# Operands and weight buffers at chosen byte offsets, another DMA order in the prologue, and two more warm-up matmuls

## The chip, the cores and the metric

The kernel runs on one core of a Trainium2 chip. The metric is the device time of one execution in microseconds (us): the median of three runs was 606.72 us, between 606.63 and 608.52. The profile was taken from another execution, which took 604.41 us.

## The reference

Attention with a soft cap over 2 x 12 heads, then two feed-forward layers over the 896 tokens, all in float32 (the weights come as float64):

```
scores = scale * (q @ k.T)                   # 448 x 448 per head, head size 64
scores = cap * tanh(scores / cap)
attn   = exp(scores - max); attn /= (sum(attn) + 1e-9)
x      = attn @ v                            # as 896 tokens x 768
x      = (x @ w_a) * (x @ w_b) @ w_out       # 768 -> 1536 -> 768
h      = max(x @ w_in, 0)                    # 768 -> 2048
out    = (h * h) @ w_out2                    # 2048 -> 768
```

## The kernel before

**Prologue.** q and k of the first of 12 pairs of heads (`qk0`), the scalar cap (`craw`), `qk1` of the second pair and the first weight unit are loaded; six matmuls on a tile of zeros (`wacc`, L517) run meanwhile. Then come the first scores, from `qk0` (L51, L57), and their Tanh (L527, L528), whose factor `c1` VectorE makes from the scalar. The engines branch on the size of the cap, and the first of two bodies runs.

**Attention.** For each pair the body computes the scores and Tanh of the next pair (L51, L57, L226, L237), Exp (L257), the product with v (L235, L270) and the sums of the exponentials (L276, L278). Each float32 matmul stands as two in the trace. The normalised result is split into two float32r tiles, a high part and the low rest, so that three float32r products give nearly float32 accuracy.

**The feed-forward layers** are 408 weight blocks of 128 x 128. For one block, `mm` (L173, L175, L177) issues six matmuls of 448 columns: the high weights with the low operand, the low weights with the high operand, and both high parts, each for the two halves of the tokens. TensorE loads 128 x 128 weights before each. The operands are the tiles x0 to x5 (144 blocks), g0 to g11 (72), y0 to y5 (96) and h0 to h14 with `hlast` (96), one operand tile per block; this gives four stages. Accumulators take turns in PSUM (`sc`, `sc`, `pd`).

**Weights.** Six blocks make a unit. A unit is loaded as float64 into one of three buffers `raw`, turned into float32 (`nar`) by VectorE and ScalarE, and split into high and low parts in one of four buffers `whl`; `tick` does this three units ahead. All engines work through their instructions in the order in which they are written; semaphores hold them back where data is missing. SP issues nearly all DMAs, in the order of its queue.

**Where tiles lie.** Tiles are laid one after the other within each partition. The tiles of the left side (th0, qk1, raw, hlast, nar, whl, then x and later y) start 32 bytes past a multiple of 256, since their sizes (12544, 3584, 6144, 7168, 3072 bytes) are multiples of 256 themselves. Those of the right side (g, and later h) are laid from the top and start 224 bytes past one.

Of the kernel before, what the change touches and what calls it, by code (L numbers as in the profile page):

```python
# [8 lines left out]
F32 = mybir.dt.float32  # L9
F32R = mybir.dt.float32r  # L10
# [7 lines left out]
B, H, S, D = 2, 12, 448, 64  # L18
DM = H * D
FF1, FF2 = 1536, 2048  # L20
P = 128
# [6 lines left out]
KD = DM // P  # L28
NF1 = FF1 // P
NF2 = FF2 // P  # L30
UB = 6
UC = UB * P
RAWB, NARB, HLB = 3, 2, 4
AHEAD = 3
WARM = 6
LOAD_AT = (0, 1, 2, 6)
CONV_AT = ((7, 8), (9,), (10,), (11,), (12,), (13, 14), (15, 16), (17,), (18,), (19,), (20,), ())
WTOP = 122876.0
EPS = 1e-9
CAP_BITS = 0x42200001  # L40
# [2 lines left out]
def f32(ap):  # L43
    return ap.bitcast(F32)
# [15 lines left out]
def fetch(nc, raws, wu, u):  # L60
    t = raws[u % RAWB]
    src = wu[u]
    if wu.dtype != F32:
        src = src.bitcast(I32).rearrange("p (n t) -> p n t", t=2)
    nc.sync.dma_start(out=t, in_=src)
    return t


def body(ctx, tc, qk, v, wu, out, c1, cabs, guard, dscr, qk1, kept, bounded):
    nc = tc.nc  # L70
    ax = ExitStack()
# [11 lines left out]
    wp = ctx.enter_context(tc.tile_pool(name="wp", bufs=1))  # L83

    th0, h_last, raws = kept
    raw_t, hl_t = {0: raws[0]}, {}
    NU = wu.shape[0]
    wide = wu.dtype != F32
    pos = {"load": 1}

    def load_units(n):
        while pos["load"] < min(n, NU):
            raw_t[pos["load"]] = fetch(nc, raws, wu, pos["load"])
            pos["load"] += 1
# [3 lines left out]
    def conv(u, step, alone=False):  # L98
        if not 0 <= u < NU:
            return  # L100
        if step == 1:
            nar_t[u] = raw_t[u]
        if step == 6:
            hl = wp.tile([P, 2, UC], F32R, tag="whl", name="whl", bufs=HLB)
            if alone:
                nc.vector.tensor_copy(hl[:, 0], nar_t[u])
            else:
                nc.scalar.activation(out=hl[:, 0], in_=nar_t[u], func=AF.Copy)  # L108
            hl_t[u] = hl
        elif step == 7:  # L110
            raw_t.pop(u)
            hl = hl_t[u]
            nc.vector.tensor_tensor(out=hl[:, 1], in0=nar_t.pop(u), in1=f32(hl[:, 0]), op=ALU.subtract)  # L113
        elif not wide:
            return
        elif step == 1:
            t = wp.tile([P, UC], F32, tag="nar", name="nar", bufs=NARB)
            nc.vector.tensor_scalar(out=t, in0=raw_t[u][:, :, 1].bitcast(F32), scalar1=WTOP, scalar2=-WTOP, op0=ALU.min, op1=ALU.max)  # L118
            nar_t[u] = t
        elif step == 2:  # L120
            t = nar_t[u]
            if alone:
                nc.vector.tensor_scalar(out=t, in0=t, scalar1=2.0 ** -112, scalar2=None, op0=ALU.mult)
            else:
                nc.scalar.activation(out=t, in_=t, func=AF.Copy, scale=2.0 ** -112)  # L125
        else:
            r, t = raw_t[u], nar_t[u].bitcast(I32)
            if step == 3:
                nc.vector.tensor_scalar(out=t, in0=t, scalar1=3, scalar2=None, op0=ALU.logical_shift_left)  # L129
            elif step == 4:  # L130
                nc.vector.scalar_tensor_tensor(out=t, in0=r[:, :, 0], scalar=29, in1=t, op0=ALU.logical_shift_right, op1=ALU.bitwise_or)  # L131
            elif step == 5:
                nc.vector.scalar_tensor_tensor(out=t, in0=r[:, :, 1], scalar=-(1 << 31), in1=t, op0=ALU.bitwise_and, op1=ALU.bitwise_or)  # L133
# [45 lines left out]
    def split(dst, src):  # L179
        pend.append(("A", lambda: nc.scalar.activation(out=dst[:, 0], in_=src, func=AF.Copy)))  # L180
        pend.append(("V", lambda: nc.vector.tensor_tensor(out=dst[:, 1], in0=src, in1=f32(dst[:, 0]), op=ALU.subtract)))

    xs = ExitStack()
    xpool = xs.enter_context(tc.tile_pool(name="xpool", bufs=1, side="left"))
    xhl = [xpool.tile([P, 2, B, S], F32R, name=f"x{i}") for i in range(KD)]

    ap = ax.enter_context(tc.tile_pool(name="ap", bufs=1, side="right"))

# [13 lines left out]
    def gtile():  # L202
        gbuf.append(gbuf.pop(0))
        return gbuf[-1]
# [136 lines left out]
    def steps(j):  # L341
        for n in CONV_AT[j]:
            conv(n // 7, n % 7 + 1, True)
# [75 lines left out]

    gx = ExitStack()  # L420
    gp = gx.enter_context(tc.tile_pool(name="gp", bufs=1, side="right"))
    ghl = [gp.tile([P, 2, B, S], F32R, name=f"g{i}") for i in range(NF1)]
    split(ghl[0], g0)
    tick(1)
    for f in range(1, NF1):
        ab = (acc(), acc())
        g = gtile()
# [8 lines left out]
    xs.close()  # L436
    yx = ExitStack()
    yp = yx.enter_context(tc.tile_pool(name="yp", bufs=1, side="left"))
    yhl = [yp.tile([P, 2, B, S], F32R, name=f"y{i}") for i in range(KD)]
    for o in range(KD):  # L440
        a = acc()
        for kk in range(NF1):
# [4 lines left out]
    gx.close()  # L447
    hx = ExitStack()
    hpool = hx.enter_context(tc.tile_pool(name="hp", bufs=1, side="right"))
    hhl = [hpool.tile([P, 2, B, S], F32R, name=f"h{i}") for i in range(NF2 - 1)]  # L450
    hhl.append(h_last)
    for f in range(NF2):
        a = acc()
        for kk in range(KD):
            mm(a, base + f * KD + kk, yhl[kk], kk == 0, kk == KD - 1)
        g = gtile()
# [6 lines left out]
    for o in range(KD):  # L463
        a = acc()
        t = gtile()
# [22 lines left out]
@with_exitstack  # L488
def tile_kernel(ctx, tc, qk, v, cap, wu, out):
    nc = tc.nc  # L490
    cp = ctx.enter_context(tc.tile_pool(name="cp", bufs=1))
    dp = ctx.enter_context(tc.tile_pool(name="dp", bufs=1, space=DRAM))
    keep = ctx.enter_context(tc.tile_pool(name="keep", bufs=1))
    dscr = dp.tile([NPAIR, 2 * S], F32, name="dscr")
    th0 = keep.tile([P, NT, S], F32, name="th0")
    qk1 = keep.tile([P, 2, S], F32, name="qk1")
    raws = [keep.tile([P, UC, 2] if wu.dtype != F32 else [P, UC], I32 if wu.dtype != F32 else F32, name=f"raw{i}") for i in range(RAWB)]
    h_last = keep.tile([P, 2, B, S], F32R, name="hlast")
    pro = ExitStack()
    wk = pro.enter_context(tc.tile_pool(name="wk", bufs=1))  # L500
    wps = pro.enter_context(tc.tile_pool(name="wps", bufs=2, space=PSUM))
    with tc.manual_schedule():
        craw, cabs, c1, small, eps = (cp.tile([P, 1], F32, name=n) for n in ("craw", "cabs", "c1", "small", "eps"))
        qk0 = wk.tile([P, 2, S], F32, name="qk0")
        nc.sync.dma_start(out=craw, in_=cap.broadcast_to([P, 1]))
        nc.scalar.dma_start(out=qk0[:, 1], in_=qk[0, :, 1])
        nc.sync.dma_start(out=qk0[:, 0], in_=qk[0, :, 0])
        nc.sync.dma_start(out=qk1, in_=qk[1])
        fetch(nc, raws, wu, 0)

        warm = wk.tile([P, 1], BF16, name="warm")
        nc.gpsimd.memset(warm, 0.0)
        nc.vector.memset(eps, EPS)
        nc.scalar.activation(out=small, in_=eps, func=AF.Tanh)
        wacc = wps.tile([P, 512], F32, name="wacc", bufs=1)
        for _ in range(WARM):
            nc.tensor.matmul(wacc, lhsT=warm.broadcast_to([P, P]), rhs=warm.broadcast_to([P, 512]), start=True, stop=True)  # L517

        nc.vector.scalar_tensor_tensor(out=cabs, in0=craw, scalar=-1.0, in1=craw, op0=ALU.mult, op1=ALU.max)
        nc.vector.reciprocal(out=c1, in_=cabs)  # L520
        nc.vector.tensor_scalar(out=c1, in0=c1, scalar1=D ** -0.5, scalar2=None, op0=ALU.mult)
        sc = [wps.tile([P, NC, 512], F32, tag="sc", name="sc") for _ in range(2)]
        tl = wps.tile([P, 512], F32, name="tl", bufs=1)
        score(nc, sc, qk0)
        score_tail(nc, tl, qk0)
        for part in range(2):
            nc.scalar.activation(out=th0[:, part * NC:(part + 1) * NC], in_=sc[part][:, :, :S], func=AF.Tanh, scale=c1)  # L527
        nc.scalar.activation(out=th0[:, NT - 1], in_=tl[:, :S], func=AF.Tanh, scale=c1)  # L528
        bits = nc.values_load(cabs[0:1, 0:1].bitcast(I32), min_val=0, max_val=0x7FFFFFFF)
        kept = (th0, h_last, raws)  # L530
        pro.close()

        def small_guard():
            nc.scalar.activation(out=small, in_=cabs, func=AF.Exp, scale=-1.0)
            nc.vector.tensor_scalar(out=small, in0=small, scalar1=EPS, scalar2=None, op0=ALU.mult)
            return small

        args = (qk, v, wu, out, c1, cabs)
        with tc.If(bits < CAP_BITS) as arm, ExitStack() as es:
            body(es, tc, *args, small_guard, dscr, qk1, kept, True)  # L540
        with arm.Else(), ExitStack() as es:
            body(es, tc, *args, lambda: eps, dscr, qk1, kept, False)
# [47 lines left out]
```

## Time and profile before

| | |
|---|---|
| median of three runs | 606.72 us |
| the profiled execution | 604.41 us |
| span from its first to its last instruction | 602.3 us |
| TensorE matmuls, busy | 589.4 us, 98% |
| TensorE weight loads, busy | 488.3 us, 81% |
| VectorE, busy | 389.7 us, 65% |
| ScalarE, busy | 239.8 us, 40% |
| DMA | 67.68 MB, mean 112 GB/s |

The span is the time between the first and the last instruction; the rest of the execution's time lies around it. Busy times of different engines lie beside each other. Matmuls are pipelined and their ends are modelled, so the start of one to the start of the next, and not the busy time, tells how fast TensorE goes. PE is TensorE, PEld its weight loads, DVE VectorE, ACT ScalarE; SPq and ACTq are the sequencers that issue DMAs.

### The profile page before, as it was taken

The numbers are of one execution on the slowest core, as the hardware profiler recorded it, in microseconds if no ns is written. First come the engines' busy times: TensorE is split into PE (matmuls) and PEld (weight loads), VectorE is DVE, ScalarE is ACT, GpSimd is POOL, SyncE is SP. The second block draws the span as 40 slices with busy tenths as digits, with TensorE's granted clock in tenths as the row PEclk, the third lists the DMA queues.
The fourth block names the chain that finished last, engine by engine and source line by source line (L and its number), as shares of the span: only waits on it lengthen the run. The fifth ranks groups of instructions, "written<-read, shape, count | busy, mean of one in ns | idle before, by whom it ended". The sixth has DMA issues, their size and how long they took to land.

```text
span 602.3 us, 7206 instructions
## 1 busy us (share of the span) xinstructions
PE 589.4 (98%) x2934; PEld 488.3 (81%) x2934; DVE 389.7 (65%) x525; ACT 239.8 (40%) x250; POOL 0.3 (0%) x5
## 2 busy tenths in 40 slices
PE   6999899999999999999999999999999999999996
PEld 2333236999999999999999999999999999999995
DVE  3778787788666666656655548777777686526400
ACT  4999880344333333322322224444444433212200
POOL 0000000000000000000000000000000000000000
PEclk9999999999999999999999999999999999999999
DMA  7344533145333333331433232333333335323001
GB/s 284 116 155 133 170 87 99 58 157 161 107 110 108 108 112 108 109 110 68 158 104 106 104 106 72 109 111 108 113 109 110 109 107 185 135 87 106 30 32 36
DMA packets 20549, 67.68 MB, mean 112 GB/s; under 512 B 6044, under 2 KB 9756, under 8 KB 20508
## 3 DMA queue, kind: packets, MB, share of 16 engines
q1 hardware_dynamic: 20076, 66.68, 33.1%
q8 instruction: 25, 0.41, 0.3%
q10 hardware_dynamic: 432, 0.46, 0.2%
q14 instruction: 16, 0.13, 0.1%
HBM read 64.26 MB, written 2.79 MB: 111 GB/s over the span
## 4 chain that ended last, share of the span: by engine, by line
PE 88%; DMA 5%; DVE 3%; SPq 1%; issue 1%; ACT 1%; DVEq 0%; ACTq 0%
PE sc L173 19%; PE sc L175 18%; PE sc L177 18%; PE pd L173 9%; PE pd L175 9%; PE pd L177 9%; DMA dscr<-rc 2%; PE sc L51 2%; PE pv L270 2%; DMA s<-dv 1%; DMA rb<-dscr 1%; DVE sm L263 1%; DMA qk<-in_qk_dram 1%; DVE sm L264 1%; PE dn L57 1%
## 5 line engine op out<-in xcount | busy, mean ns | idle before, releaser
L108 ACT ACTIVATE whl<-nar 128x768 fp32r<-128x768 f32 x65 | 55.1, 848 | 181.4 <-DVE nar L133 154.9
L113 DVE TENSOR_TENSOR whl<-nar,whl 128x768 fp32r<-128x768 f32 x68 | 65.2, 958 | 39.7 <-ACT whl L108 39.6
L131 DVE SCALAR_TENSOR_TENSOR nar<-raw,nar 128x768 int32<-128x768 int32 x68 | 65.1, 958 | 2.3
L133 DVE SCALAR_TENSOR_TENSOR nar<-raw,nar 128x768 int32<-128x768 int32 x68 | 64.9, 955 | 1.4
L125 ACT ACTIVATE nar<-nar 128x768 f32<-128x768 f32 x65 | 54.2, 834 | 22.4 <-DVE nar L118 22.4
L173 PE MATMUL sc<-x,whl 128*128 128x448 f32 x192 | 57.3, 369 | 0.0
L175 PE MATMUL sc<-x,whl 128*128 128x448 f32 x192 | 57.1, 368 | 0.0
L177 PE MATMUL sc<-x,whl 128*128 128x448 f32 x192 | 57.0, 368 | 0.0
L129 DVE TENSOR_SCALAR nar<-nar 128x768 int32<-128x768 int32 x68 | 37.6, 553 | 17.8 <-ACT nar L125 17.5
L118 DVE TENSOR_SCALAR nar<-raw 128x768 f32<-128x768 f32 x68 | 37.6, 552 | 4.5 <-PE tl L57 4.5
L173 PEld LDWEIGHTS sc<-x,whl 128*128 128x128 f32 x192 | 36.0, 188 | 5.1 <-issue 1.4
L175 PEld LDWEIGHTS sc<-x,whl 128*128 128x128 f32 x192 | 36.0, 188 | 3.6
L177 PEld LDWEIGHTS sc<-x,whl 128*128 128x128 f32 x192 | 36.0, 188 | 3.6
L175 PE MATMUL sc<-y,whl 128*128 128x448 f32 x132 | 38.0, 368 | 0.0
L173 PE MATMUL sc<-y,whl 128*128 128x448 f32 x132 | 37.9, 368 | 0.0
L177 PE MATMUL sc<-y,whl 128*128 128x448 f32 x132 | 37.9, 368 | 0.0
L173 PE MATMUL sc<-h,whl 128*128 128x448 f32 x120 | 36.6, 365 | 0.0
L175 PE MATMUL sc<-h,whl 128*128 128x448 f32 x120 | 36.4, 364 | 0.0
L177 PE MATMUL sc<-h,whl 128*128 128x448 f32 x120 | 36.2, 362 | 0.0
L51 PE MATMUL sc<-qk 64*128 64x448 f32 x144 | 32.0, 579 | 3.6 <-DMA qk<-in_qk_dram 2.2
L257 ACT ACTIVATE pe<-th,cabs 128x3136 f32<-128x3136 f32 x12 | 34.9, 2910 | 0.4
L226 ACT ACTIVATE th<-sc,c 128x1344 f32<-128x1344 f32 x22 | 29.2, 1376 | 6.8 <-PE sc L51 6.8
(122 smaller groups left out, 995.5 us busy)
## 6 DMA issues: line engine op xcount, KB each, us to landing
raw<-in_wu_dram SPq DMA_DIRECT2D x68, 768.0 KB, 4.2
qk<-in_qk_dram SPq DMA_DIRECT2D x11, 448.0 KB, 3.7
vt<-in_v_dram SPq DMA_DIRECT2D x12, 224.0 KB, 4.2
rb<-dscr SPq DMA_DIRECT2D x22, 112.0 KB, 3.0
out_dram<-th SPq DMA_DIRECT2D x5, 448.0 KB
s<-dv SPq DMA_DIRECT2D x22, 3.5 KB
qk<-in_qk_dram ACTq DMA_DIRECT2D x1, 224.0 KB
qk<-in_qk_dram SPq DMA_DIRECT2D x1, 224.0 KB
```

The lines of the kernel that those rows point to most:

```text
L51: nc.tensor.matmul(banks[n // NC][:, n % NC, :S], lhsT=qk[r, 1, c * P:(c + 1) * P], rhs=qk[r, 0], start=True, stop=True)
L108: nc.scalar.activation(out=hl[:, 0], in_=nar_t[u], func=AF.Copy)
L113: nc.vector.tensor_tensor(out=hl[:, 1], in0=nar_t.pop(u), in1=f32(hl[:, 0]), op=ALU.subtract)
L118: nc.vector.tensor_scalar(out=t, in0=raw_t[u][:, :, 1].bitcast(F32), scalar1=WTOP, scalar2=-WTOP, op0=ALU.min, op1=ALU.max)
L125: nc.scalar.activation(out=t, in_=t, func=AF.Copy, scale=2.0 ** -112)
L129: nc.vector.tensor_scalar(out=t, in0=t, scalar1=3, scalar2=None, op0=ALU.logical_shift_left)
L131: nc.vector.scalar_tensor_tensor(out=t, in0=r[:, :, 0], scalar=29, in1=t, op0=ALU.logical_shift_right, op1=ALU.bitwise_or)
L133: nc.vector.scalar_tensor_tensor(out=t, in0=r[:, :, 1], scalar=-(1 << 31), in1=t, op0=ALU.bitwise_and, op1=ALU.bitwise_or)
L173: nc.tensor.matmul(o[:, b, :S], lhsT=hi, rhs=m[:, 1, b], start=first, stop=False)
L175: nc.tensor.matmul(o[:, b, :S], lhsT=lo, rhs=m[:, 0, b], start=False, stop=False)
L177: nc.tensor.matmul(o[:, b, :S], lhsT=hi, rhs=m[:, 0, b], start=False, stop=last)
L257: nc.scalar.activation(out=pe, in_=th, func=AF.Exp, scale=cabs)
```

## The change

The tiles of x, y, g, h and the four weight buffers get gaps in front of them (`placed`, and the loop over HLAT), so that each starts at its own offset modulo 256. The th0 tile and what follows it move to a multiple of 256 (`lead`); qk1 has no tile of its own any more and lies in the third raw buffer. The weight buffers are four fixed tiles in place of a rotating pool.

```
-WARM = 6
+WARM = 8
+LINE = 256
+XAT, YAT, HLAT = (0, 32, 64, 96, 128, 192), (0, 224, 160, 64, 128, 32), (0, 32, 64, 128)

+def placed(pool, name, cur, at):
+    tiles = []
+    for i, a in enumerate(at):
+        gap = (a - cur) % LINE
+        if gap:
+            pool.tile([P, gap // 4], F32, name=f"{name}gap{i}")
+        tiles.append(pool.tile([P, 2, B, S], F32R, name=f"{name}{i}"))
+        cur = a
+    return tiles

+    cur = 0
+    whl = []
+    for i, a in enumerate(HLAT):
+        if a - cur:
+            wp.tile([P, (a - cur) // 4], F32, name=f"whlgap{i}")
+        whl.append(wp.tile([P, 2, UC], F32R, name=f"whl{i}"))
+        cur = a
...
-            hl = wp.tile([P, 2, UC], F32R, tag="whl", name="whl", bufs=HLB)
+            hl = whl[u % HLB]
-    xhl = [xpool.tile([P, 2, B, S], F32R, name=f"x{i}") for i in range(KD)]
+    xhl = placed(xpool, "x", HLAT[-1], XAT)
-    ghl = [gp.tile([P, 2, B, S], F32R, name=f"g{i}") for i in range(NF1)]
+    ghl = placed(gp, "g", 0, [32 * i % LINE for i in range(1, NF1 + 1)])
-    yhl = [yp.tile([P, 2, B, S], F32R, name=f"y{i}") for i in range(KD)]
+    yhl = placed(yp, "y", HLAT[-1], YAT)
-    hhl = [hpool.tile([P, 2, B, S], F32R, name=f"h{i}") for i in range(NF2 - 1)]
+    hhl = placed(hpool, "h", 0, [32 * i % LINE for i in range(1, NF2)])
...
+    keep.tile([P, 56], F32, name="lead")
     th0 = keep.tile([P, NT, S], F32, name="th0")
-    qk1 = keep.tile([P, 2, S], F32, name="qk1")
     raws = [...]
+    if wu.dtype != F32:
+        qk1 = raws[2].rearrange("p n t -> p (n t)")[:, :2 * S].bitcast(F32).rearrange("p (t s) -> p t s", t=2)
...
+        nc.sync.dma_start(out=qk0[:, 0], in_=qk[0, :, 0])
+        nc.scalar.dma_start(out=qk0[:, 1], in_=qk[0, :, 1])
         nc.sync.dma_start(out=craw, in_=cap.broadcast_to([P, 1]))
-        nc.scalar.dma_start(out=qk0[:, 1], in_=qk[0, :, 1])
-        nc.sync.dma_start(out=qk0[:, 0], in_=qk[0, :, 0])
         nc.sync.dma_start(out=qk1, in_=qk[1])
```

In the built program x0 to x5 lie at 0, 32, 64, 96, 128 and 192 past a multiple of 256, y0 to y5 at 0, 224, 160, 64, 128 and 32, and whl0 to whl3 at 0, 32, 64 and 128. The tiles g0 to g11 lie at 128, 160, 192, 224, 0, 32 and so on in steps of 32, h0 to h14 at 32, 64, 96 and so on, and hlast at 0.

Two places show where instructions move. The first is the start of SP's queue (qk0 is the first pair's tile, whose q half SP loads; craw is the scalar; qk1, later raw2, takes the second pair). Before:

```order
L505 DMA craw_78<-in_cap_dram 128x1
L507 DMA qk0_83<-in_qk_dram 128x448
L508 DMA qk1_65<-in_qk_dram 128x896
L65 DMA raw0_66<-in_wu_dram 128x1536
L529 TENSOR_LOAD cabs_79
```

and after:

```order
L529 DMA qk0_83<-in_qk_dram 128x448
L531 DMA craw_78<-in_cap_dram 128x1
L532 DMA raw2_68<-in_qk_dram 128x896
L67 DMA raw0_66<-in_wu_dram 128x1536
L553 TENSOR_LOAD cabs_79
```

The scalar and q have changed places, and the second pair goes into raw2; the rest of the queue stands as before.

The second place is TensorE at the end of the warm-up (wacc is its accumulator; the numbers at qk and raw tell tiles apart). Before:

```order
L517 LDWEIGHTS warm
L517 MATMUL wacc<-warm 128x512
L51 MATMUL sc<-qk_83 128x448 x6
L57 MATMUL tl<-qk_83 64x448 x2
L529 TENSOR_LOAD cabs
L539 COMPARE_AND_BRANCH
L51 MATMUL sc<-qk_65 128x448 x6
```

and after:

```order
L541 LDWEIGHTS warm
L541 MATMUL wacc<-warm 128x512
L53 MATMUL sc<-qk_83 128x448 x6
L59 MATMUL tl<-qk_83 64x448 x2
L553 TENSOR_LOAD cabs
L563 COMPARE_AND_BRANCH
L53 MATMUL sc<-raw_68 128x448 x6
```

Eight pairs of such weight loads and matmuls stand ahead of the first scores in place of six, and the second pair's scores read raw2; all else on TensorE, VectorE and ScalarE keeps its order.

## Rows read from the trace of the kernel before

**Rows 1.** The page's busy line: engine, busy us, share of the span, instructions.

```profile
PE 589.4 (98%) x2934; PEld 488.3 (81%) x2934; DVE 389.7 (65%) x525; ACT 239.8 (40%) x250; POOL 0.3 (0%) x5
```

**Rows 2.** The page's chain that ended last, by engine.

```profile
PE 88%; DMA 5%; DVE 3%; SPq 1%; issue 1%; ACT 1%; DVEq 0%; ACTq 0%
```

**Rows 3.** Longest of TensorE's waits: us in total, times, longest.

```profile
PE dn L57 <- DVE dv L285: 2.5, 2, 2.2
```

**Rows 4.** Stages x, g, y, h: length; busy (instructions) by engine; clock, DMA share, GB/s.

```profile
98.90:273.90 175.00, 175.00 (x849) 158.94 (x848) 121.04 (x153) 58.21 (x71) 0.00 (x0) 1.00 0.33 110
273.90:361.20 87.30, 87.30 (x433) 80.94 (x432) 53.42 (x67) 24.64 (x30) 0.00 (x0) 1.00 0.32 109
361.20:480.20 119.00, 119.00 (x577) 108.08 (x576) 92.12 (x111) 54.48 (x63) 0.00 (x0) 1.00 0.31 101
480.20:596.80 116.60, 116.60 (x577) 107.84 (x576) 53.50 (x69) 27.49 (x34) 0.00 (x0) 1.00 0.27 95
```

**Rows 5.** TensorE in order of time, stage x: start, length, instruction, count.

```profile
149.85 0.57 PE L173 MATMUL sc<-x,whl 128*128 128x448 f32 x2
...
151.09 0.57 PE L173 MATMUL sc<-x,whl 128*128 128x448 f32 x2
```

**Rows 6.** The same view in stage h, around hlast; first matmuls of blocks.

```profile
497.23 0.57 PE L173 MATMUL sc<-h,whl 128*128 128x448 f32 x2
...
498.44 0.57 PE L173 MATMUL sc<-hlast,whl 128*128 128x448 f32 x2
...
499.68 0.57 PE L173 MATMUL pd<-h,whl 128*128 128x448 f32 x2
...
500.89 0.57 PE L173 MATMUL pd<-h,whl 128*128 128x448 f32 x2
```

**Rows 7.** The same view in the last output, after its hlast.

```profile
587.33 0.36 PE L175 MATMUL sc<-h,whl 128*128 128x448 f32 x1
...
587.73 0.37 PE L173 MATMUL sc<-h,whl 128*128 128x448 f32 x1
```

**Rows 8.** Pair 1's tail scores, and SP's load of weight unit 2.

```profile
14.84 0.97 PE L57 MATMUL dn<-qk 64*64 64x448 f32 x4
...
22.98 0.43 SPq L65 DMA_DIRECT2D raw<-in_wu_dram  x1
```

**Rows 9.** All engines in order of time, prologue; idle time before and its releaser.

```profile
0.74 0.39 SPq L505 DMA_DIRECT2D craw<-in_cap_dram  x1
...
0.89 2.74 PE L517 MATMUL wacc<-warm 128*128 128x512 bf16 x6 [0.89 <-POOL warm L512]
...
1.19 0.42 SPq L507 DMA_DIRECT2D qk<-in_qk_dram  x1
...
5.23 0.15 DVE L521 TENSOR_SCALAR c<-c 128x1 f32<-128x1 f32 x1
...
5.79 4.21 PE L51 MATMUL sc<-qk 64*128 64x448 f32 x12 [2.16 <-DMA qk<-in_qk_dram]
...
9.15 2.65 ACT L527 ACTIVATE th<-sc,c 128x1344 f32<-128x1344 f32 x2 [6.48 <-PE sc L51]
...
12.38 2.53 PE L51 MATMUL sc<-qk 64*128 64x448 f32 x12 [1.49 <-ACT th L528]
```

**Rows 10.** TensorE's weight loads for the scores of pairs 0 and 1.

```profile
6.67 0.37 PEld L51 LDWEIGHTS sc<-qk 64*128 64x128 f32 x2 [0.38 <-issue]
...
8.91 0.36 PEld L51 LDWEIGHTS sc<-qk 64*128 64x128 f32 x2 [0.38 <-issue]
...
12.86 0.19 PEld L51 LDWEIGHTS sc<-qk 64*128 64x128 f32 x2 [0.18 <-issue]
...
13.99 0.19 PEld L51 LDWEIGHTS sc<-qk 64*128 64x128 f32 x2 [0.18 <-issue]
```

More of the change, by code (lines that the diff above doesn't have):

```diff
@@ L494, in tile_kernel @@
     dscr = dp.tile([NPAIR, 2 * S], F32, name="dscr")
+    keep.tile([P, 56], F32, name="lead")
     th0 = keep.tile([P, NT, S], F32, name="th0")
-    qk1 = keep.tile([P, 2, S], F32, name="qk1")
     raws = [keep.tile([P, UC, 2] if wu.dtype != F32 else [P, UC], I32 if wu.dtype != F32 else F32, name=f"raw{i}") for i in range(RAWB)]
+    if wu.dtype != F32:
+        qk1 = raws[2].rearrange("p n t -> p (n t)")[:, :2 * S].bitcast(F32).rearrange("p (t s) -> p t s", t=2)
+    else:
+        qk1 = keep.tile([P, 2, S], F32, name="qk1")
     h_last = keep.tile([P, 2, B, S], F32R, name="hlast")
```

## The prediction

> **What bounds the kernel now.** I read the busy times first, then the chain, then TensorE's waits, and only then the spacing of single matmuls. The busy row [rows 1] gives TensorE 98% of the span, VectorE 65% and ScalarE 40%, and the chain [rows 2] lies on TensorE for 88%. The reader is to see that almost nothing is left to win by removing waits: the longest things TensorE ever waits for are 2.5 us of VectorE work in the attention part [rows 3], 2.16 us for the first q and k and 1.49 us for a Tanh [rows 9]. So the time goes down only if the matmuls themselves follow each other faster, or if the prologue gets shorter.
>
> "Busy" does not say how fast matmuls follow each other, since their ends are modelled and overlap. The spacing of starts does. I call one 128x128 weight block with its six matmuls (three products, two halves of the tokens) a block; the four stages have 144 (operand x), 72 (g), 96 (y) and 96 (h, six of them hlast), 408 in all. From the stage table [rows 4], leaving out the 18 matmuls of x that ran before it: x 175.0 us / 846 matmuls = 0.2069 us, g 87.3 / 432 = 0.2021, y 119.0 / 576 = 0.2066, h 116.6 / 576 = 0.2024. Matmuls of one shape, at one granted clock (1.00), with no idle time, have two paces: 1.24 us per block for x and y, 1.21 for g and h. Single starts show the same: x goes from 149.85 to 151.09, 1.24 [rows 5].
>
> What differs between the stages is where the operand lies. In the kernel before, every weight buffer, x, y and hlast start 32 bytes past a multiple of 256, and g and h 224 bytes past one. I call (operand minus weight address) modulo 256 the distance: it is 0 for x, y and hlast and 192 for g and h. The stages differ in other things too (VectorE is busy 69% of stage x and 46% of stage h [rows 4]), but hlast separates them: it is the sixteenth operand of the h stage, in the midst of h tiles, with the same engines working beside it. Its block runs from 498.44 to 499.68, 1.24 us, and the h blocks before and after it take 498.44 - 497.23 = 1.21 and 500.89 - 499.68 = 1.21 [rows 6]. So the pace changes at once with the tile, and back.
>
> [...]
>
> **The change part by part.**
>
> 1. *Placement.* No instruction of the 408 blocks is added, removed or moved. The weight buffers now lie at 0, 32, 64 and 128, and each operand has its own place. Counted through the loops, about 58 blocks run at distance 0, 54 at 192, and 296 at the six other multiples of 32, which no row of before shows; the distance also changes from one block to the next, where before it stood still for a whole stage. Before: 246 blocks x 1.24 + 162 x 1.2125 = 305.0 + 196.4 = 501.5 us, a mean of 1.229. After: distance 0, 58 x 1.24 = 71.9; distance 192, 54 x 1.21 = 65.3; the other 296 are unknown. From below they are bounded by the columns: the fp32 scores of the attention part stream 448 columns twice per step in 13.99 - 12.86 = 1.13 us for three steps, 0.377 each or 0.188 per 448 columns [rows 10], which gives 1.13 per block. From above I mirror the known gain: distance 192 is 0.03 faster than distance 0, so one that is 0.03 slower makes 1.27. I take 1.20, the nearest spacing that the trace has after a change of distance: going from hlast to h in the last output, the starts 587.33 and 587.73 lie two matmuls apart, 0.20 each [rows 7]. 296 x 1.20 = 355.2; together 492.4 us, 9.1 less. With 1.13 it would be 29.8 less, with 1.27 11.6 more.
>
> [...]
>
> 2. *Cover for a faster TensorE.* In stage x VectorE has 121.04 us of work in 175.0 and the DMA engines are busy a third of the time at 110 GB/s [rows 4]. At 1.20 per block both loads grow by 3%, and neither becomes the bound. That work costs nothing unless a block falls below about 0.86 us, where VectorE would be full.
>
> 3. *q first, then the scalar.* SP issues q at 1.19 now and the scalar at 0.74 [rows 9]; these change places, so q starts 0.45 us earlier. The first score waits for q and k [rows 9], and k stays where it was. Bounds 0 (k or the shared DMA engines set the time) and 0.45; I take 0.4, nearer the row. The scalar feeds c1, ready at 5.38 now, so at about 5.8 then; Tanh asks for it at 9.15 [rows 9], and even with the fastest start below not before about 7.3. That is cover enough. SP's branch and the loads behind it wait for the same scalar and slip by as much, with the first v needed only after the second pair's scores.
>
> 4. *Two more warm-up matmuls.* Six take 2.74 us from 0.89 [rows 9], so eight end near 4.5, and the gap until the first score falls from 2.16 us to about 0.9. The first scores run at half pace: four weight loads from 6.67 to 8.91 lie 0.75 apart, those from 12.86 to 13.99 0.377 [rows 10], though the column of the granted clock reads 1.00. [...] If the higher level stood from the first score on, the first Tanh would start 4 x 0.37 = 1.5 us earlier; if nothing changes, 0. No row shows eight warm-ups; I take 0.5, because the six, with a gap behind them, did not bring it. There is no loss below nothing, since they are over before q is there.
>
> Parts 3 and 4 together are 0.9 us (0 to 2.0). They pass to the end: the second pair's scores wait for that Tanh [rows 9], and after them TensorE stands still for little more than those 2.5 us.
>
> 5. *qk1 in a weight buffer.* The second pair's q and k go into raw2, so the load of weight unit 2 must wait until the scores and tails of pair 1 have read it. These tails run at 14.84 to 15.81, and that load is issued at 22.98 [rows 8]: 7 us of slack, no cost. What is late next there is the order of the queue itself, which is unchanged.
>
> Sum: 604.41 (the profiled execution's own time, 2.1 us of it lie outside the 602.3 us span) - 9.1 - 0.9 = 594.4. That execution was 2.3 us faster than the median of the runs, 606.72, so the median after is 594.4 + 2.3 = 596.7 us.
>
> **The rivals.**
>
> A. *The collisions go altogether.* If the pace is lost to reads that meet and the new places keep them apart, blocks fall towards 1.13. For it: the scores reach 0.188. Against: 58 blocks still lie at distance 0, and each fast stage still loses 0.015 per matmul. All 350 others at 1.13 give 71.9 + 395.5 = 467.4, 34 less: 572 us; halfway, 587.
>
> B. *The pace isn't set by placement, or the new distances average out to the present mean.* [...] For the second: of eight distances only two are known, and both paces could be typical. Against the first: hlast. Then only the prologue stays, 606.7 - 0.9 = 605.8 us.
>
> C. *Worse distances.* The place is every block whose operand and weights now meet more often than at distance 0; before, the pace settled down within a stage, and a distance that changes with each block may restart a slow beginning each time. Price: at 1.27 in the 296 blocks, 11.6 more, less 0.9: 617.4 us. It decides from a mean over the 408 blocks of 1.229 + (0.9 + 1.8) / 408 = 1.236. For it: two of the eight distances already differ by 2.5% [rows 6], and no row caps the other six from above. Against: every change to 192 that the rows show is fast at once.
>
> D. *The placement does not come out as the diff says*, because a pool rounds or shifts tiles. The sizes (7168, 6144, 12544) are multiples of 256 and the gaps multiples of 32, so I give it almost nothing; its time is that of B.
>
> **How the numbers follow.** 0.3% is 1.8 us, about what a measurement of this kernel can tell from no change. Forecast: 0.54, with its own range 591 to 603 (the 296 blocks at 1.185 to 1.22, the prologue 2.0 to 0). A: 0.16, all below 591. B with D: 0.19, from 603 to 608.5, half of it within 0.3% and the rest faster. C: 0.11. Faster 0.54 + 0.16 + 0.09 = 0.79, the same 0.10, slower 0.11. The range for 8 in 10 leaves out the fast half of A and most of C: 587 to 607.
>
> **What would show it.** In the changed kernel's stage table, x and y near 0.200 to 0.203 us per matmul and g and h at 0.200 to 0.203 as well; blocks of one stage differ among themselves, and x0 with the weight buffer at 0 still has 1.24. The first score starts near 5.4, and the weight loads behind it are 0.75 apart only for one or two steps. It would be wrong if x and y still show 0.2067 (rival B), if g and h rise above 0.2045 (rival C), or if all stages fall under 0.197 (rival A). If the first Tanh starts at 9.15 as before, the prologue's 0.9 us are not there.

## The result and the profile after

The changed kernel takes 601.63 us (median of four runs, 600.09 to 602.29) against 607.62 us (606.63 to 608.53) for the kernel before: a ratio of 0.990, 95% interval 0.987 to 0.993. That is 6.0 us faster where 10.0 were forecast; the time forecast was 596.7 us in a range of 587 to 607. The profiled execution took 602.29 us, 2.1 less than the profiled one of before.

The stage table of the changed kernel (stages x, g, y, h from first matmul to the next stage's first; columns as in [rows 4]):

```profile
100.33:272.43 172.10, 172.10 (x848) 158.91 (x847) 120.81 (x153) 58.24 (x71) 0.00 (x0) 1.00 0.33 112
272.43:360.37 87.94, 87.94 (x433) 81.07 (x432) 53.41 (x67) 24.65 (x30) 0.00 (x0) 1.00 0.31 108
360.37:477.48 117.11, 117.11 (x577) 108.11 (x576) 92.14 (x111) 54.42 (x63) 0.00 (x0) 1.00 0.30 103
477.48:594.66 117.18, 117.18 (x577) 107.95 (x575) 53.50 (x69) 27.49 (x34) 0.00 (x0) 1.00 0.27 95
```

Divided by 846, 432, 576 and 576 matmuls, all four stages now go at 203.4, 203.6, 203.3 and 203.4 ns per matmul. Before, x and y took 206.9 and 206.6, and g and h 202.1 and 202.4 [rows 4]. So two stages became faster and two slower, and the four together take 494.3 us against 497.9: 3.6 us less. VectorE has the same work in each stage as before.

The prologue and the start of the attention part, all engines in order of time (to compare with [rows 9]):

```profile
0.74 0.39 SPq L529 DMA_DIRECT2D qk<-in_qk_dram  x1
...
0.89 3.59 PE L541 MATMUL wacc<-warm 128*128 128x512 bf16 x8 [0.89 <-POOL warm L536]
...
1.19 0.42 SPq L531 DMA_DIRECT2D craw<-in_cap_dram  x1
...
4.42 2.71 PE L53 MATMUL sc<-qk 64*128 64x448 f32 x12
...
6.72 0.15 DVE L545 TENSOR_SCALAR c<-c 128x1 f32<-128x1 f32 x1
...
6.97 2.65 ACT L551 ACTIVATE th<-sc,c 128x1344 f32<-128x1344 f32 x2 [4.30 <-DVE c L545]
...
10.20 3.47 PE L53 MATMUL sc<-raw 64*128 64x448 f32 x12 [2.18 <-ACT th L552]
...
15.21 2.48 PE L290 MATMUL pv<-pe,vt 128*64 128x448 f32 x12
```

The first scores start 1.37 us earlier and take 2.71 us in place of 4.21; the second pair's start 2.18 us earlier. Yet those last 3.47 us against 2.53, and the first weight block starts at 91.55 us, where before it started at 89.40. Its first matmul, before and after:

```profile
89.40 0.47 PE L173 MATMUL sc<-x,whl 128*128 128x448 f32 x1
```

```profile
91.55 0.47 PE L193 MATMUL sc<-x,whl 128*128 128x448 f32 x1
```

The granted clock tells part of it (stretch, TensorE busy, clock, DMA share, GB/s). After:

```profile
4.40:10.20 5.80, 3.62 (x17) 1.00 0.81 278
10.20:13.60 3.40, 3.40 (x12) 0.71 0.87 265
13.60:17.00 3.40, 3.40 (x20) 0.79 0.93 369
```

Before, in the second of these stretches:

```profile
10.20:13.60 3.40, 1.91 (x10) 1.00 1.03 398
```

TensorE has stood still for 2.18 us until 10.20, and from 11.64 to 15.06 us the granted clock is 0.50. Another part lies later: TensorE's wait on VectorE in the attention part, 2.5 us before [rows 3], is longer in this execution, and behind it the clock is 0.50 once more, from 73.09 to 76.50 us (0.88 on average from 66 to 80 us, 1.00 before):

```profile
PE dn L59 <- DVE dv L305: 4.1, 2, 3.7
```

### The profile page after: what moved, and what is told of

Read it like the earlier page. It is cut to its first block, busy times and chain, and to the rows that moved or that the text cites. A ratio compares the mean times of both kernels' runs of the same rounds, so it can differ in the third digit from the quotient of the medians.

```text
span 600.1 us, 7210 instructions
## 1 busy us (share of the span) xinstructions
PE 587.4 (98%) x2936; PEld 488.5 (81%) x2936; DVE 390.1 (65%) x525; ACT 239.8 (40%) x250; POOL 0.3 (0%) x5
## 4 chain that ended last, share of the span: by engine, by line
PE 92%; DMA 4%; DVE 2%; SPq 1%; issue 0%; ACT 0%; DVEq 0%
PE sc L193 19%; PE sc L195 19%; PE sc L197 19%; PE pd L195 9%; PE pd L197 9%; PE pd L193 9%; PE pv L290 3%; PE sc L53 2%; DMA dscr<-rc 2%; DMA raw<-in_wu_dram 1%; PE dn L296 1%; PE dn L59 1%; DMA rb<-dscr 1%; SPq L339 0%; SPq L230 0%
## 5 line engine op out<-in xcount | busy, mean ns | idle before, releaser
L193 PE MATMUL sc<-x,whl 128*128 128x448 f32 x192 | 56.6, 366 | 0.0
L195 PE MATMUL sc<-x,whl 128*128 128x448 f32 x192 | 56.6, 366 | 0.0
L197 PE MATMUL sc<-x,whl 128*128 128x448 f32 x192 | 56.5, 365 | 0.0
L290 PE MATMUL pv<-pe,vt 128*64 128x448 f32 x144 | 31.2, 571 | 0.0
```

Of the source, the lines that this page charges most:

```text
L193: nc.tensor.matmul(o[:, b, :S], lhsT=hi, rhs=m[:, 1, b], start=first, stop=False)
L195: nc.tensor.matmul(o[:, b, :S], lhsT=lo, rhs=m[:, 0, b], start=False, stop=False)
L197: nc.tensor.matmul(o[:, b, :S], lhsT=hi, rhs=m[:, 0, b], start=False, stop=last)
L290: nc.tensor.matmul(pvt[j][(1 - i) * D:(2 - i) * D, :S], lhsT=vt[:, n], rhs=pe[:, n], start=False, stop=c == NC - 1)
```

## The experiments

"Distance" is operand minus weight address modulo 256, as in the prediction.

**e1_place_only** is the changed kernel with the prologue of before:

```
-WARM = 8
+WARM = 6
...
+        nc.sync.dma_start(out=craw, in_=cap.broadcast_to([P, 1]))
...
-        nc.sync.dma_start(out=craw, in_=cap.broadcast_to([P, 1]))
```

> The placement of the change with the prologue of before (six warm-ups, scalar first). If the gain is the placement's, the 408 blocks take 502.9 us from first to last matmul start as in the changed kernel's profile (before: 507.2), and the kernel gains about 4.3 us, ratio 0.993. If most of the measured 6 us comes from the prologue, it gains under 2 us, ratio above 0.997.

Measured: ratio 0.996 (0.992 to 1.000), the medians 3.7 us apart, and the blocks from first to last start take 502.9 us, to 0.01 us the value of the changed kernel. The stages go at 203.4, 203.6, 203.3 and 203.4 ns again. The placement alone gives the 3.6 us in the stages, and it gave them in both profiled executions that had it.

**e2_prologue_only** is the kernel before with the other half:

```
-WARM = 6
+WARM = 8
...
+        nc.sync.dma_start(out=qk0[:, 0], in_=qk[0, :, 0])
+        nc.scalar.dma_start(out=qk0[:, 1], in_=qk[0, :, 1])
         nc.sync.dma_start(out=craw, in_=cap.broadcast_to([P, 1]))
-        nc.scalar.dma_start(out=qk0[:, 1], in_=qk[0, :, 1])
-        nc.sync.dma_start(out=qk0[:, 0], in_=qk[0, :, 0])
```

> The kernel before with the prologue of the change alone (q, k, scalar; eight warm-ups). Placement theory: the blocks stay at 507.2 us, x 0.2067 and g 0.2022 per matmul; the second pair's scores start near 10.2 us instead of 12.4, and what of these 2.2 us reaches the end is between 0 and 2.2, ratio 0.996 to 1.000. Rival (the prologue is the larger half of the gain): ratio 0.993 to 0.995.

Measured: ratio 1.000 (0.997 to 1.002). The second pair's scores start at 10.06 us, and no gain is to be seen at the end (the interval leaves room for 1.6 us at most). The blocks keep the old paces.

**e3_distances_32_to_128** and **e4_distances_160_224_0** give each stage one constant distance, by a gap of DX or DY bytes ahead of x and y, one behind g and h, and one of DH ahead of hlast with 256 - DH behind it, so that the weights stay 32 bytes past a multiple of 256 (the lines for y, h and hlast and the helper `shifted`, which lays the gap, are left out here):

```
+DX, DG, DY, DH = 32, 64, 96, 128        # e4: 160, 0, 224, 64
...
-    xhl = [xpool.tile([P, 2, B, S], F32R, name=f"x{i}") for i in range(KD)]
+    xhl = shifted(xpool, "x", KD, front=DX)
...
-    ghl = [gp.tile([P, 2, B, S], F32R, name=f"g{i}") for i in range(NF1)]
+    ghl = shifted(gp, "g", NF1, back=(192 - DG) % 256)
```

> The kernel before with one constant distance (operand minus weight address modulo 256) per stage: x 32, g 64, y 96, h and hlast 128. Theory 1 (the pace follows the distance of operand and weights alone): per matmul about what these distances show among the mixed ones of the changed kernel, x 204.2, g 201.1, y 205.0, h 202.9 ns. Theory 2 (a distance that stands still locks TensorE into a slow pattern, whatever it is): all stages between 202 and 207 ns, none under 202. Theory 3 (the side of memory or the stage sets the pace): x and y stay at 206.7, g and h at 202.2 ns.

> As the run with 32 to 128, with x 160, g 0, y 224, h and hlast 64. Theory 1: x 203.4, g 206.7 (as slow as x and y before), y 203.8, h 201.1 ns. Theory 2: none under 202 ns. Theory 3: x and y 206.7, g and h 202.2 ns.

Measured in stages x, g, y, h: 200.1, 200.0, 205.3, 204.0 ns for 32, 64, 96, 128, and 200.2, 202.7, 204.4, 200.0 for 160, 0, 224, 64 (169.31 us / 846 and so on). The kernels took 598.86 and 598.64 us in one execution each. Theory 3 falls: x goes at 200. Theory 2 falls as it was put: 200.0 is faster than any pace of before. Theory 1 holds within about 1 ns for 64, 96, 128 and 224. But constant 32 and 160 are 3 to 4 ns faster than among the mixed distances, where they take 204.2 and 203.4, and distance 0 in g takes 202.7, not 206.7. In all runs of constant distance the weights lie at 32, so these runs alone can't tell the distance from the operand's own offset. The changed kernel's trace can: with weights at 0, 32, 64 and 128, its blocks at distance 64 average 200.9, 200.7, 201.5 and 200.9 ns per matmul, while those with the operand at offset 64 average 200.9, 204.5, 204.4 and 201.9. So the pace goes with the distance rather than with the operand's own place.

**e5_before_again** is the kernel before, unchanged, for a second profile.

> The kernel before once more, for a second profile of it. If its profiled execution above (604.41 us) was a lucky one, this profile shows the same 507.2 us for the blocks, but the first block of stage x starts near 92 us in place of 89.4, with a longer wait of TensorE on VectorE in the attention part and a stretch at half the clock behind it, as the four runs so far do. If it was typical, the first block starts near 89.4 again.

Measured: 604.40 us, first block at 90.15 us, the longest wait on VectorE 3.6 us, no stretch at half the clock behind it (the mean granted clock of the span is 0.998, as in the first profile); between the two readings. It also holds an observation that bears on all the others. TensorE in order of time, two of the 18 matmuls of x that run ahead of the stage, and then two at the start of the stage itself:

```profile
90.65 0.36 PE L177 MATMUL sc<-x,whl 128*128 128x448 f32 x1
...
93.49 0.36 PE L175 MATMUL sc<-x,whl 128*128 128x448 f32 x1
```

```profile
99.25 0.36 PE L175 MATMUL sc<-x,whl 128*128 128x448 f32 x1
...
100.90 0.37 PE L173 MATMUL sc<-x,whl 128*128 128x448 f32 x1
```

14 spacings in 2.84 us are 202.9 ns each; 8 in 1.65 us are 206.3. The same three lines of the kernel, the same operands, the same distance 0 (the weights are of the next unit), and after the 5 us in between another pace, which then stays for the whole stage. In the first profile of this kernel the same 14 spacings, of the same matmuls, took 2.90 us, 207 each:

```profile
89.91 0.37 PE L177 MATMUL sc<-x,whl 128*128 128x448 f32 x1
...
92.81 0.37 PE L175 MATMUL sc<-x,whl 128*128 128x448 f32 x1
```

So a distance does not have one pace. The four stages, on the other hand, went at the same paces in all three profiles of this placement (the first, e2 and e5: 174.94 to 175.00 us in x, 87.30 to 87.35 in g, 119.00 to 119.04 in y, 116.59 to 116.60 in h).

**e6_good_distances** takes the paces of 32 and 64 at their word (DX, DG, DY, DH = 32, 64, 32, 64), and **e9_good_distances_again** is the same kernel once more.

> The kernel before with a constant distance of 32 for x and y and 64 for g, h and hlast, the prologue as before. If the pace follows the distance, every stage goes at 200.0 ns per matmul, the 408 blocks take 489.5 us (507.2 before, 502.9 with the mixed distances of the change), and the kernel gains 17 us over before: ratio 0.971 to 0.974. If the paces seen at 32 and 64 hung on the neighbouring stages, some stage goes at 202 ns or more and the ratio is above 0.975.

> The run with 32 for x and y and 64 for g, h and hlast once more, unchanged. Theory 4 (a distance that stands still lets a stage settle into one of several patterns, and which one is decided when the stage is entered, by chance or by the code ahead): at 32 stage x may go at 200.0 (as in the run with 32 to 128) or at 206.6 ns (as in the first run of this kernel), different from that run; at 64 g and h go at 200.0 as in all five stages so far. Theory 5 (the pattern is fixed by the program): exactly the first run's paces, x 206.6, y 206.7, g and h 200.0 ns.

Measured: e6 0.993 (0.990 to 0.997), far from 0.972; its 12 runs lie between 596.96 and 605.79 us. Stage x of e6's profile and of e9's, which took 597.71 us:

```profile
101.34:276.27 174.93, 174.93 (x848) 159.16 (x847) 121.08 (x153) 58.24 (x71) 0.00 (x0) 1.00 0.32 110
```

```profile
100.21:269.52 169.31, 169.31 (x848) 158.89 (x847) 120.98 (x153) 58.24 (x71) 0.00 (x0) 1.00 0.34 114
```

One program, the same engine work beside it, and 206.8 ns per matmul in one execution, 200.1 in the other: 5.6 us in this stage alone. Theory 5 falls and theory 4 stands, with one reserve: e6 and e9 ran on different chips, so this pair alone doesn't rule the chip out as the cause. Against that, e6's own 12 runs on one chip spread over 8.8 us, and in e5 two paces stand in one execution. At 32, y was slow in both (206.7), and at 64 g and h went at 200.0 in both.

**e7_384_columns** asks what the 200 ns consist of. It leaves the last 64 columns of each half out of most block matmuls (the lines of the first product are left out here):

```
+W = 384
...
+        w0 = S if first else W
...
-            nc.tensor.matmul(o[:, b, :S], lhsT=lo, rhs=m[:, 0, b], ...)
+            nc.tensor.matmul(o[:, b, :W], lhsT=lo, rhs=m[:, 0, b, :W], ...)
```

> Distances x 32, g 192, y 0, h 64, and all block matmuls but the first product of each accumulation have 384 columns in place of 448 (the last 64 columns of each half are left out of them). The columns are 26.7 ns less at the higher clock. If the operand's stream with its stalls sets the pace, x and h fall to about 173 ns, g to 175, y to 180. If 200 ns is the time that a 128-column weight load needs until its matmul may start, x and h stay at 200 ns, and y and g come down to about 200 too.

Measured: h 173.9, g 175.6, y 175.2 ns (x has 1.93 us of new waits in it and is left out). The weight loads are recorded with 188 ns, longer than these spacings, so the recorded loads overlap, and loads of 188 ns one behind the other are not the bound. The line of stage h:

```profile
431.81:531.97 100.16, 100.16 (x577) 99.83 (x576) 53.52 (x69) 27.52 (x35) 0.00 (x0) 1.00 0.32 112
```

In h, 26.1 ns are gone against the 200.0 that the same distance took with 448 columns (e4), both at a granted clock of 1.00. Each accumulation's first product keeps its 448, so 62.7 columns are missing in the mean: 0.417 ns for each, 26.7 for 64. The scores stream twice 448 columns in 0.377 us, 0.420 ns each [rows 10]. So the pace falls with the columns, as the first reading has it. By an estimate from these two figures 448 columns are 187 to 188 ns, and 12 to 13 ns lie over the columns in h in both runs. Distance 0, slow with 448 columns (18 to 20 ns over them by the same estimate), isn't slow with 384 (12 to 14 ns); whether the width does this or another pattern was met in this one execution stays open.

**e8_x0_g0** has x 0, g 0, y 160, h 64.

> Distances x 0, g 0, y 160, h 64. In the run with g at 0, stage g went at 202.66 ns, though x and y at 0 take 206.67. If the pattern depends on how a stage is entered, g, entered from x at distance 0, keeps 206.67 ns here. If the modulus is larger than 256 or the side of memory counts, g goes at 202.66 again. y at 160: 200.2 as x did there, or another pace by the same two readings.

Measured: x 202.8, g 202.7, y 206.7, h 200.0 ns. At 0 x went at 202.8 here and at 206.9 in the kernel before, and y at 160 at 206.7, where x had 200.2. The side of memory can't explain that, since x is where it was; x and its weights both stand 256 bytes further, so a larger modulus of their own addresses isn't excluded by this run alone, but in e5 nothing had moved at all.

**e10_all_64** is the kernel before with distance 64 everywhere, the one fast distance that had the same pace in every stage so far. **e11_all_64_prologue** adds the change's prologue, and **e12_all_64_filled** keeps TensorE busy in its pause:

```
+        for _ in range(FILL):        # 9
+            nc.tensor.matmul(wacc, lhsT=warm.broadcast_to([P, P]), rhs=warm.broadcast_to([P, 512]), ...)
```

> The kernel before with the one distance 64 in all four stages, prologue as before. If 64 has only one pattern, every stage goes at 200.0 ns, the blocks take 489.5 us, and the kernel gains about 16 us over before: ratio 0.972 to 0.976. If 64 has slow patterns too, x or y go at 203 to 207 ns, the times of single runs spread by several us, and the ratio is above 0.98.

> All distances 64 with the prologue of the change (q, k, scalar; eight warm-ups). As the prologue alone brought 0.9996, the same as the run with all at 64, within 0.002. If the prologue gains what its early scores suggest, 2 us less.

> As the run before, with nine more matmuls on the tile of zeros between the first pair's tail scores and the second pair's scores, where TensorE stands still for 2.2 us in the changed kernel. If the clock falls because of that pause, and the 3.4 us at half pace that follow in the changed kernel's profile swallow the prologue's gain, the granted clock stays at 1.00 from the first scores on, pair 1's product with v starts near 13.8 us in place of 15.2, and the kernel gains 1 to 2 us over the run without them. If something else swallows it, nothing changes.

Measured: 0.980 (0.976 to 0.985), 0.981 (0.977 to 0.984) and 0.980 (0.976 to 0.984), medians 593.90, 594.28 and 593.86 us. All stages of all three go at 200.0 to 200.1 ns; e10:

```profile
100.03:269.34 169.31, 169.31 (x848) 158.73 (x847) 120.80 (x153) 58.23 (x71) 0.00 (x0) 1.00 0.33 114
269.34:355.74 86.40, 86.40 (x433) 81.00 (x432) 53.43 (x67) 24.64 (x30) 0.00 (x0) 1.00 0.32 110
355.74:470.94 115.20, 115.20 (x577) 108.00 (x576) 92.17 (x111) 54.45 (x63) 0.00 (x0) 1.00 0.31 104
470.94:586.14 115.20, 115.20 (x577) 107.81 (x575) 53.52 (x69) 27.48 (x34) 0.00 (x0) 1.00 0.27 97
```

These are 486.1 us for the stages, 8.2 less than with the change's placement. This version beats the kernel before; it wasn't run beside the changed kernel, but all 18 runs of the three lie between 591.90 and 597.10 us, below the 600.09 to 602.29 of that one. The ratio fell short of the 0.972 to 0.976 expected, because the 489.5 us expected for the blocks are 2448 matmuls at 200.0 ns and leave out the pause of about 5 us between the 18 that run ahead and the stage, which the 507.2 us of before contain. The 11.8 us of gain in the stages on 606.3 us are 0.981.

The prologue shows no gain a third time. In e12 the clock stays up, as expected (columns as in the table of the clock above):

```profile
10.20:13.60 3.40, 3.40 (x20) 1.00 0.91 291
13.60:17.00 3.40, 2.82 (x16) 1.00 0.89 357
```

But the gain ends elsewhere. TensorE and VectorE in order of time:

```profile
7.78 2.14 PE L542 MATMUL wacc<-warm 128*128 128x512 bf16 x9
10.10 2.53 PE L53 MATMUL sc<-qk 64*128 64x448 f32 x12 [0.19 <-ACT th L545]
...
13.95 2.48 PE L281 MATMUL pv<-pe,vt 128*64 128x448 f32 x12
17.73 0.57 PE L287 MATMUL dn<-sm,ones 128*32 128x448 f32 x2 [1.30 <-DVE sm L275]
```

```profile
10.07 0.56 DVE L129 TENSOR_SCALAR nar<-raw 128x768 f32<-128x768 f32 x1 [2.21 <-DMA raw<-in_wu_dram]
...
14.44 0.96 DVE L124 TENSOR_TENSOR whl<-nar,whl 128x768 fp32r<-128x768 f32 x1
15.31 0.15 DVE L552 TENSOR_SCALAR small<-small 128x1 f32<-128x1 f32 x1
15.38 1.08 DVE L274 TENSOR_TENSOR sm<-pe 128x896 f32<-128x896 f32 x1
```

The product with v is 1.26 us earlier than in the changed kernel, near the 13.8 expected, but then TensorE waits 1.30 us for VectorE's sums of the first pair. Ahead of the sums VectorE has the conversion of weight unit 0, which waits until 10.07 us for its load and starts its last step at 14.44; the sums start behind it, at 15.38. In the changed kernel, without the filler, the time at a granted clock of 0.50 covers most of that wait (0.26 us of it are left).

This isn't the whole loss. With the old prologue, in e10, the same matmul on the sums starts about 1 us later than the 17.73 us of e12 and the 17.67 of e11:

```profile
18.71 0.57 PE L286 MATMUL dn<-sm,ones 128*32 128x448 f32 x2 [0.78 <-DVE sm L274]
```

So about 1 us of lead gets past the clock and past unit 0. At the first weight block it is gone or nearly so: 91.26 us in e10, 91.90 in e11, 90.92 in e12. In between TensorE waits 3.4, 4.7 and 3.3 us for VectorE's copy `dv`. Ahead of the longest of these waits VectorE waits for the reciprocals (`rc`), which go to DRAM and back; SP issues that trip 0.5 us behind a weight unit of 768 KB. From the chain that ended last, before and after the change:

```profile
61.09 5.03 DMA dscr<-rc
```

```profile
60.43 6.67 DMA dscr<-rc
```

The changed kernel starts this trip 0.66 us earlier and gets it back 1 us later. It takes 6.4 us in e5, the second profile of before, as well, so its length isn't the change's doing. That it swallows the lead is read from the traces; no run tests it.

## Why the prediction was right or wrong

- **What bounds the kernel: right.** The gain is in the spacing of matmuls, and hlast was the right witness that the place of a tile matters. With no instruction changed in the stages, they took 497.9, 494.3 and 486.1 us by placement alone, so the first half of rival B falls. That reads of operand and weights meet, as rival A supposes, was not shown; what the changed kernel's trace shows is that the pace goes with the distance between the two places (200.7 to 201.5 ns at distance 64, wherever the weights lie).
- **One pace per distance: wrong.** But for hlast's blocks each stage of before showed one pace from its start to its end (in g 202.2 ns in each sixth of the stage), and the prediction took it for the distance's own. e5 shows 202.9 and 206.3 ns at distance 0, e6 and e9 show 206.8 and 200.1 at 32.
- **The size of the placement term: wrong, 3.6 us for 9.1.** The failing number is 1.20 us per block for the 296 blocks at unknown distances. Averaged over the changed kernel's spacings, 32, 64, 96, 128, 160 and 224 take 204.2, 201.1, 205.0, 202.9, 203.4 and 203.8 ns; their mean of 203.4 is 1.220 per block, 296 x 0.020 = 6 us more. I had misread the row that it comes from. After hlast the spacings at distance 192 repeat in threes, 207, 199 and 201 ns, and the two between 587.33 and 587.73 leave the long one out. Over the next nine spacings, from 587.73 [rows 7] to 589.55 (the line below this list), the pace is 1.82 us / 9 = 202.2 ns, the old one of 192. Nor was it a row of any of the six distances in question. The known terms were close: 1.227 for 1.24 at distance 0, 1.213 for 1.21 at 192.
- **Cover for a faster TensorE: right.** VectorE's work stays where it was; at 200 ns nothing new waits. The margin is smaller than the 0.86 us per block of the prediction, though: in e7 stage x has two new waits, 1.3 us on ScalarE and 0.6 on VectorE, at 1.07 us per block.
- **q first and the warm-ups: larger at their place, nothing at the end.** The scores start at 4.42 us (5.4 forecast), right behind the warm-ups, and from 5.08 us on their weight loads lie 0.377 us apart, the pace that part 4 calls the higher level. The start is 1.37 us earlier, where q alone was given 0 to 0.45. The scalar was not covered: c1 is ready at 6.87 us (5.8 forecast), and the first Tanh waits for it until 6.97. "They pass to the end" is the step that failed: of the 2.18 us at the first Tanh 0.7 are left at the first pair's sums on TensorE (17.95 us, 18.66 before). The 3.4 us at a granted clock of 0.50 behind the pause take most of the rest; with the pause filled, VectorE's wait for unit 0 does. Of the 1 us that e12 has there against e10, 0.3 us reach the first weight block, too little to show in the time.
- **qk1 in a weight buffer: right.** Unit 2's load is issued at 23.06 us, 22.98 before [rows 8].
- **Rivals.** B's second half, an average of the distances, came close: 203.4 ns against a mean of 204.9 before. A and C did not happen. A's "halfway, 587" is 589 by its own 572 and B's 605.8.
- **What stays open.** The stages explain 3.6 of the 6.0 us measured. The kernel before scatters from 599.8 to 609.0 us over 51 runs in all these comparisons, and its median of 607.6 against the change comes from four; in the other three comparisons it was 606.3 to 606.8. The interval of that comparison (4.4 to 7.9 us) and that of e1 (0.2 to 4.8 us) meet only between 4.4 and 4.8, somewhat over 3.6. No run settles where the rest lies. Nor is the scatter traced to the patterns: the three profiles of that placement have the same stage paces, and their first weight blocks start at 89.40, 93.43 and 90.15 us. The first of them, from which the prediction was worked out, is the earliest of all. What decides the pattern on entering a stage stays open too.

The kernel before, TensorE in order of time, nine spacings behind the last line of [rows 7]:

```profile
589.55 0.37 PE L173 MATMUL sc<-h,whl 128*128 128x448 f32 x1
```

## What to carry to other kernels

Stage x, all equal matmuls, ran at 206.8 and at 200.1 ns per matmul in two executions without one idle gap (e6, e9); look at the spacing of starts, stage by stage, and at tiles that differ in place alone. Mixing the distances, as the change does, gave the same average in both profiled executions (203.3 to 203.6 ns); one distance with a single fast pattern, here 64 (200.0 to 200.1 ns), is better, and has to be shown in several stages and executions before it is believed. An early gain has to be followed through every wait behind it before it is counted: here 2.18 us at the second pair's scores were 0.7 at the first pair's sums.

## What the runs showed of the hardware that was not expected

- One program goes at 206.8 or 200.1 ns per matmul in the same stage in two executions (e6, e9), and at 202.9 and 206.3 ns before and after a pause in one execution (e5). The first of these two was 207 in another execution of the same program.
- At distance 64 the spacing was 200.0 to 200.1 ns in all 19 stages of eight runs that had it with 448 columns; at 0 it was 206.9, 206.6, 202.8 and 202.7.
- Weight loads recorded with 188 ns stand one to a matmul, and the matmuls follow each other every 174 ns (e7, stage h).
- In the changed kernel, behind a pause of 2.18 us, TensorE's granted clock was 0.50 for 3.4 of the next 6.8 us (0.71 and 0.79 on average over two stretches); with the pause filled it stayed at 1.00 (e12).
